# Retention and a two-layer ELU network on one Trainium2 core: the second token block's second matrix product, from one Strassen level to two

## The chip, the cores and the metric

The kernel runs on one core of a Trainium2 chip (trn2). The metric is the device time of one execution in microseconds; several executions are timed and the median is given. A profile is taken of one execution. In it, PE is TensorE (PEld its weight loads), DVE is VectorE, ACT is ScalarE, POOL is GpSimd, and SP is SyncE, which here issues all DMAs, in the order in which they stand in the program.

## The reference

Everything is fp32. First a recurrent retention over 4 sequences of 768 tokens with 8 heads of 64, then a network without biases:

```python
for t in range(S):
    state = gamma * state + outer(k[t], v[t])
    y[t] = q[t] @ state / sqrt(D)
x = y.transpose(0, 2, 1, 3).reshape(3072, 512)
h = x @ w_in                          # 512 -> 2048
g = where(h > 0, h, exp(min(h, 0)) - 1)
out = g @ w_out                       # 2048 -> 512
```

The state is one 64x64 matrix per head, gamma one number per head.

## The kernel before

**Blocks.** The 3,072 tokens are worked on in six blocks of 512, numbered 0 to 5. For each block the retention is computed in chunks (masked scores L274, states L305, outputs L339 and L365), which leaves the block's input x, turned, in `xb`. Then come the first matrix product (w_in), the ELU on ScalarE and VectorE (L419 to L423), and the second product (w_out). The retention of a block is cut into five steps (`retention_step`), which are put between the matrix products of the block before it.

**Products.** Block 0 multiplies plainly (`plain_first`, `plain_second`). Block 1 uses one Strassen-Winograd level in both products: 7 products of half-size matrices instead of 8, in the order 1, 2, 6, 7, 5, 3, 4. `first` does it for w_in, in four parts n; `second` for w_out, each product with 16 matmuls of 128x128 weights and 256 columns (32 records in the trace, since an fp32 matmul leaves two). Blocks 2 to 5 use two levels in the second product (`second_twice`: 7 x 7 = 49 products of 4 matmuls, 128 columns each, 8 records) and in two of the seven products of the first (`first_twice`).

**Weights.** They come as 16 pieces of float64 bits. `prepare` (ScalarE) and `decode` (VectorE, four operations) turn them to fp32. Pieces 0 to 7 are w_in and stay in SBUF. Pieces 8 to 15 are w_out and pass through the four slots of `w_s` while block 0 multiplies with them in `plain_second`; piece 12 takes the slot of piece 8, and so on. Pieces are loaded three ahead in a pool `stage` of three tiles: `load_piece` is called at the end of each decode. For each piece, VectorE also makes the four sums of one Strassen level, `so` (L471 to L476), and the decoded piece and `so` are stored to a DRAM scratch of 32 quarter matrices (`quarters`, L176 and L477).

**The weights of two levels.** `second` fetches each of its seven weight matrices back from that scratch (`fetch`, tile `ws`, 1 MB, three in flight, in `stage`), multiplies, and lets VectorE make the four second-level sums of the same matrix (`combine_w_out`, L594 to L600, 512 columns each), which are stored to `scratch2` for blocks 2 to 5. For w_in, GpSimd makes such sums for two matrices during block 1's first product (`combine_small`, L678, stored to `scratch3`).

**The ring.** Two-level products take their weights from a ring of 11 tiles `wq` of 256 KB; `fetch_small` issues the next fetch when a tile has been used. The ring takes the memory of the pools `stage` and `t4`, which are closed first; this is done in `change`, behind the last product of block 1's second product.

**Order.** The schedule is by hand: each engine executes its instructions in program order. Generators (`first`, `second`, ...) yield between products, and the main program decides what stands between. PSUM: banks "a" (two buffers), "b" and "d" (one each), and four for the rest. Output tiles of block 0 are in `gq["T3"]` (`g_out`), which is otherwise an input of the second product from block 1 on. The output sums of one-level products lie in `hpool`, copies of PSUM in `mpool`, four tiles each.

Of the kernel before, what the change touches and what calls it, by code (L numbers as in the profile page):

```python
# [17 lines left out]
def kernel(  # L18
# [70 lines left out]
    gq["T1"] = gq["C12"]  # L89
    four = lambda x: gq[x].rearrange("p (i a) t -> p i (a t)", a=2)  # L90
    g_plain = [four(x)[:, i, :] for x in gnames[:4] for i in range(4)]
    g_out = [gq["T3"][:, 2 * i : 2 * i + 2, :] for i in range(4)]


    chunks = [divmod(m, NCH) for m in range(NCHUNK)]
# [51 lines left out]

    quarters = lambda f: scratch.rearrange("(s k) p (f c) -> k f p s c", k=2, f=4)[f // 4, f % 4]  # L150

    def decode(fine=False):

# [305 lines left out]
    def plain_second():  # L459

        ops = [bank(x).rearrange("p a b -> p (a b)") for x in "aabd"]
        for f in range(NF):
            wo = decoded[2 * NQ + f]
            for row in range(2):
                for d in range(4):
                    nc.tensor.matmul(  # L466
                        ops[d], lhsT=wo[:, row, d * P : (d + 1) * P], rhs=g_plain[row * NF + f],
                        start=(f == 0 and row == 0), stop=(f == NF - 1 and row == 1),
                    )
            so = t4.tile([P, 4, 256], FP32, name="so", tag="t4")  # L470
            tt = lambda o, x, y, op: nc.vector.tensor_tensor(out=o, in0=x, in1=y, op=op)  # L471
            a11, a21, a12, a22 = (wo[:, r, 256 * d : 256 * d + 256] for r in range(2) for d in range(2))
            tt(so[:, 0], a21, a22, ALU.add)
            tt(so[:, 1], so[:, 0], a11, ALU.subtract)
            tt(so[:, 2], a11, a21, ALU.subtract)
            tt(so[:, 3], a12, so[:, 1], ALU.subtract)  # L476
            nc.sync.dma_start(quarters(f)[:, 8:16], so.rearrange("p a (d c) -> p (a d) c", c=P))  # L477
            yield
        for d in range(4):
            ot = g_out[d]  # L480
            eng = (nc.scalar.copy, nc.vector.tensor_copy)[d % 2]
            eng(ot.rearrange("p a b -> p (a b)"), ops[d])
            nc.sync.dma_start(out[0, d // 2, :, :, d % 2, :].rearrange("t p c -> p t c"), ot)

    def combine_w_in(n):

# [82 lines left out]
        return strassen(product, use, None)  # L569


    SLOT = {1: 0, 2: 2, 3: 7, 4: 3, 5: 4, 6: 5, 7: 6}
    ORDER2 = [1, 2, 6, 7, 5, 3, 4]
    fetched = {}

    def fetch(tb, j):
        t = stage.tile([P, 4, 4, P], FP32, name="ws", tag="stage")
        nc.sync.dma_start(
            t.rearrange("p q f c -> p q (f c)"), scratch[4 * SLOT[j] : 4 * SLOT[j] + 4].rearrange("q p x -> p q x")
        )  # L580
        fetched[tb, j] = t

    INPUT2 = {1: "C11", 2: "C21", 3: "C22", 4: "C11", 5: "T1", 6: "C11", 7: "T3"}

    def next_input(j):

        x, op = {2: ("T3", ALU.add), 6: ("C21", ALU.subtract)}[j]
        for n in range(NQ):
            q = slice(2 * n, 2 * n + 2)
            nc.vector.tensor_tensor(out=gq["C11"][:, q], in0=gq[x][:, q], in1=gq["C11"][:, q], op=op)  # L590

    def combine_w_out(j, ws):

        tt = lambda o, x, y, op: nc.vector.tensor_tensor(out=o, in0=x, in1=y, op=op)  # L594
        a11, a12, a21, a22 = (ws[:, q] for q in range(4))
        s12, s34 = (t4.tile([P, 2, 4, P], FP32, name="so", tag="t4") for _ in range(2))
        tt(s12[:, 0], a21, a22, ALU.add)
        tt(s12[:, 1], s12[:, 0], a11, ALU.subtract)
        tt(s34[:, 0], a11, a21, ALU.subtract)
        tt(s34[:, 1], a12, s12[:, 1], ALU.subtract)  # L600
        for k, x in enumerate((s12, s34)):
            nc.sync.dma_start(
                scratch2[j - 1, :, 1024 * k : 1024 * k + 1024], x.rearrange("p k f d -> p (k f d)")
            )

    def second(tb, behind_last):
        def product(j, ps, begin):
            ws = fetched.pop((tb, j))
            for f in range(NF):
                for d in range(2):  # L610
                    nc.tensor.matmul(  # L611
                        ps[:, d, :], lhsT=ws[:, 2 * d + f // 4, f % 4, :], rhs=gq[INPUT2[j]][:, f, :],
                        start=(begin and f == 0 and d == 0), stop=(f == NF - 1), skip_group_check=True,
                    )
            at = ORDER2.index(j) + 3
            if j in (2, 6):
                next_input(j)
            combine_w_out(j, ws)
            if at < 7:
                fetch(tb, ORDER2[at])  # L620
            if j == 4:
                behind_last()

        def use(name, h):
            r, t = int(name[1]) - 1, int(name[2]) - 1
            if name == "C12":
                ot = hpool.tile([P, 2, TH], FP32, name="h", tag="h")
                nc.scalar.copy(ot, h)
                h = ot
            nc.sync.dma_start(out[tb, r, t].rearrange("p d c -> p (d c)"), h.rearrange("p d c -> p (d c)"))  # L630

        return strassen(product, use, None)

    RING = 11
    TWICE = [2, 3]
    SMALL = {5: 0, 6: 1, 7: 2, 3: 3}
    small_w, to_fetch, before = [], [], []
    for tb in range(2, NTB):  # L640
        for j in TWICE:
            m1, m2, *mine = [(tb, 0, j, k) for k in (1, 2, 6, 7, 5, 4, 3)]
            to_fetch += [m1] + before[:1] + [m2] + mine[:2] + before[1:] + mine[2:3]
            before = mine[3:]
        to_fetch, before = to_fetch + before, []
        for j in ORDER2:
            last = (4, 3) if j == 4 and tb == NTB - 1 else (3, 4)
            mine = [(tb, 1, j, k) for k in (1, 2, 6, 7, 5) + last]
            to_fetch += mine[:2] + before + mine[2:5]
            before = mine[5:]  # L650
        to_fetch, before = to_fetch + before, []
    to_fetch = [x for x in to_fetch if x[1] == 1 or x[3] in SMALL]

    def fetch_small():
        if not to_fetch:
            return
        name = to_fetch.pop(0)
        _, which, j, k = name
        t = ring.tile([P, 4, P], FP32, name="wq", tag="wq")
        if k in SMALL:  # L660
            n = SMALL[k]
            nc.sync.dma_start(
                t.rearrange("p f d -> p (f d)"), (scratch3, scratch2)[which][j - 1, :, 512 * n : 512 * n + 512]
            )
        else:
            q = 4 * SLOT[j] + {1: 0, 2: 1, 4: 3}[k]
            nc.sync.dma_start(t.rearrange("p f d -> p (f d)"), scratch[q])
        small_w.append((name, t))
# [4 lines left out]
    def combine_small(j):  # L673

        t = stage.tile([P, 4, 4, P], FP32, name="wi", tag="stage")
        a11, a12, a21, a22 = (W_IN[j][:, 2 * r : 2 * r + 2, :, c, :] for r in range(2) for c in range(2))
        s1, s2, s3, s4 = (t[:, k].rearrange("p (n f) c -> p n f c", f=2) for k in range(4))
        tt = lambda o, x, y, op: nc.gpsimd.tensor_tensor(out=o, in0=x, in1=y, op=op)  # L678
        tt(s1, a21, a22, ALU.add)
        tt(s2, s1, a11, ALU.subtract)  # L680
        tt(s3, a11, a21, ALU.subtract)
        tt(s4, a12, s2, ALU.subtract)
        nc.sync.dma_start(scratch3[j - 1], t.rearrange("p k f d -> p (k f d)"))

    xs = {}

# [11 lines left out]
    def combine_x_twice():  # L698

        t = tpool.tile([P, 4, 2, 2, P], FP32, name="ts", tag="ts")  # L700
        b = [xb[:, 2 + k].rearrange("p (h t c) -> p t h c", h=2, t=2)[:, u] for k in range(2) for u in range(2)]
        for _ in quarters_of_input(t[:, :, 0], *b):
            pass
        for n, j in enumerate(TWICE):
            b11, b12, b21, b22 = (x[:, n] for x in b)
            s1, s2, s3, s4 = (t[:, k, 0, n] for k in range(4))
            xs[j] = {1: b11, 2: b21, 3: b22, 4: s4, 5: s1, 6: s2, 7: s3}
# [82 lines left out]
        return lambda: elu(g, g, 3, combine if name == "C22" else None)  # L790

    def second_twice(tb, behind_last):
        quarter = lambda x, r, t: x[:, 4 * r : 4 * r + 4, P * t : P * t + P]
        ts, kept2 = {}, {}

        def inputs(j):
# [250 lines left out]
    for n in range(NQ):  # L1047
# [14 lines left out]
        tail = cur  # L1062
        for j in smalls[n]:
            combine_small(j)
    for j in ORDER2[:3]:
        fetch(1, j)
    for m in range(2 * CPB, 3 * CPB):
        scale_v(m)

    def change():  # L1070

        nonlocal ring, tpool
        early.close()
        ring = ctx.enter_context(tc.tile_pool(name="ring", bufs=RING))
        tpool = ctx.enter_context(tc.tile_pool(name="tpool", bufs=2))
        for _ in range(RING):
            fetch_small()
        combine_x_twice()

    cur = second(1, change)  # L1080
    next(cur)
    next(cur)
    for _ in tail:
        pass
    flush()
    for step, s in enumerate(cur):
        retention_step(2, step)


    tail = iter(())  # L1090
    for tb in range(2, NTB):
        more = tb + 1 < NTB
        qa, qd, u2, end = {}, {}, {}, None
# [140 lines left out]
```

## Time and profile before

| | us |
|---|---|
| median of 5 executions | 650.88 (650.2 to 653.25) |
| the profiled execution | 653.25 |
| its span | 651.5 |
| TensorE busy | 635.2 (98%) |
| VectorE busy | 470.0 (72%) |
| ScalarE busy | 235.4 (36%) |
| GpSimd busy | 39.6 (6%) |
| mean DMA rate over the span | 206 GB/s |

The stages, as TensorE's instructions show them in the profiled execution: block 0's second product from 80.8 to 144.9, block 1's first product from there, block 1's second from 189.8 to 250.9 (with the last two products of the first and with block 2's retention between), block 2 from there to 354.3. The chain of work that ended last is followed back from the last instruction, at each step to what released it. "Issue" is time in which the engine waited for nothing that the profile shows. A line of a timeline has the start, the duration from the first start to the last end, the engine, the source line, the operation, its output and input tiles and how many instructions are merged in it; in brackets stands the idle time before it and what ended that. A window line has the bounds, the length, the busy time of TensorE, of its weight loads, VectorE, ScalarE and GpSimd with instruction counts, TensorE's clock as a share of full speed, the busy share of the DMA engines, and GB/s.

### The profile page before, as it was taken

How to read it: one execution, taken by the hardware profiler on the slowest of the kernel's cores; microseconds unless marked ns; L12 is line 12 of the kernel's file. 1: busy time of each engine (PE TensorE's matmuls, PEld its weight loads, DVE VectorE, ACT ScalarE, POOL GpSimd, SP SyncE). 2: the span in 40 equal slices, each digit the busy share in tenths (PEclk: the TensorE clock that was granted, in tenths of full speed). 3: DMA queues.
4: the chain of work that ended last, by engine and by line, in shares of the span. 5: the costliest groups of instructions: out<-in, count | busy, mean ns of one | idle time of the engine just before them, and what ended most of it. 6: DMA issues, size and time to landing. Idle time of an engine off the chain costs nothing.

```text
span 651.5 us, 15272 instructions
## 1 busy us (share of the span) xinstructions
PE 635.2 (98%) x6344; PEld 542.5 (83%) x6344; DVE 470.0 (72%) x830; ACT 235.4 (36%) x439; POOL 39.6 (6%) x38
## 2 busy tenths in 40 slices
PE   4999999999999999999989999999999999999998
PEld 3774445458888889989989988999988999988997
DVE  5689778667866636599757578958569958557976
ACT  6477542005441001546111455311355311256311
POOL 1001100000720000110000020000020000000000
PEclk9999999999999999999989999999999999999999
DMA  8648987546384766912768830688850588610694
GB/s 340 244 138 320 330 238 234 143 133 211 123 297 162 258 228 216 384 65 63 257 207 270 295 157 3 205 270 283 274 214 3 178 264 267 225 55 1 209 305 166
DMA packets 69013, 134.16 MB, mean 206 GB/s; under 512 B 5713, under 2 KB 23505, under 8 KB 66641
## 3 DMA queue, kind: packets, MB, share of 16 engines
q1 hardware_dynamic: 68944, 133.19, 60.6%
q8 instruction: 50, 0.82, 0.5%
q14 instruction: 19, 0.15, 0.1%
HBM read 109.05 MB, written 24.12 MB: 204 GB/s over the span
## 4 chain that ended last, share of the span: by engine, by line
PE 96%; DVE 1%; ACT 1%; DMA 1%; issue 1%; POOL 0%; SPq 0%; POOLq 0%
PE pa L812 16%; PE pa L773 10%; PE pd L812 8%; PE hp L452 6%; PE pa L466 4%; PE pa L611 4%; PE pb L812 4%; PE pb L773 4%; PE pa L553 4%; PE pa L727 4%; PE qa L773 3%; PE y L339 2%; PE pd L611 2%; PE qd L773 2%; PE pd L553 2%; PE pd L773 2%
## 5 line engine op out<-in xcount | busy, mean ns | idle before, releaser
L820 ACT COPY ms<-pa 128x128 f32<-128x128 f32 x83 | 22.0, 265 | 116.2 <-PE pa L812 116.2
L420 ACT ACTIVATE r<-r 128x512 f32<-128x512 f32 x96 | 60.5, 630 | 3.0
L812 PE MATMUL pa<-ts,wq 128*128 128x128 f32 x448 | 59.2, 275 | 0.0
L812 PE MATMUL pd<-ts,wq 128*128 128x128 f32 x440 | 58.2, 275 | 0.0
L812 PEld LDWEIGHTS pa<-ts,wq 128*128 128x128 f32 x448 | 54.8, 192 | 0.2
L812 PEld LDWEIGHTS pd<-ts,wq 128*128 128x128 f32 x440 | 53.5, 192 | 0.2 <-DVE res L824 0.2
L419 ACT ACTIVATE r<-gC 128x512 f32<-128x512 f32 x64 | 39.9, 624 | 33.9 <-DVE gC L781 33.9
L812 PE MATMUL pa<-gC,wq 128*128 128x128 f32 x384 | 52.2, 279 | 0.0
L812 PEld LDWEIGHTS pa<-gC,wq 128*128 128x128 f32 x384 | 47.7, 193 | 1.0
L248 POOL TENSOR_TENSOR kvn<-kvn,vf 128x512 f32<-128x512 f32 x22 | 25.6, 1168 | 359.4 <-DMA kvn<-in_qkv_dram 263.0
L423 DVE SCALAR_TENSOR_TENSOR gC<-r,gC 128x512 f32<-128x512 f32 x64 | 45.9, 749 | 0.7 <-ACT r L420 0.7
L503 ACT COPY m<-pa 128x512 f32<-128x512 f32 x27 | 15.7, 581 | 60.7 <-PE pa L611 35.5
L824 DVE TENSOR_TENSOR res<-pd,ms 128x128 f32<-128x128 f32 x54 | 15.4, 285 | 29.3 <-PE pd L812 28.7
L689 DVE TENSOR_TENSOR ts<-gC,ts 128x512 f32<-128x512 f32 x48 | 33.0, 688 | 0.8
L689 DVE TENSOR_TENSOR ts<-gC 128x512 f32<-128x512 f32 x48 | 32.8, 682 | 0.0
L466 PE MATMUL pa<-gC,w_s 128*128 128x512 f32 x64 | 30.6, 600 | 0.0
L611 PE MATMUL pa<-gC,ws 128*128 128x256 f32 x128 | 28.6, 381 | 0.0
L812 PE MATMUL pb<-gC,wq 128*128 128x128 f32 x192 | 27.3, 283 | 0.1
L611 PEld LDWEIGHTS pa<-gC,ws 128*128 128x128 f32 x128 | 24.1, 190 | 3.4
L812 PEld LDWEIGHTS pb<-gC,wq 128*128 128x128 f32 x192 | 24.5, 198 | 0.8 <-DVE gC L423 0.8
L845 ACT COPY res<-pa 128x128 f32<-128x128 f32 x27 | 7.2, 265 | 45.8 <-PE pa L812 45.8
L781 DVE TENSOR_TENSOR gC<-qa,gC 128x512 f32<-128x512 f32 x8 | 5.5, 691 | 25.1 <-PE qa L773 18.3
(206 smaller groups left out, 1298.1 us busy)
## 6 DMA issues: line engine op xcount, KB each, us to landing
wq<-scratch_dram SPq DMA_DIRECT2D x228, 256.0 KB, 4.3
wraw<-in_w_dram SPq DMA_DIRECT2D x16, 1024.0 KB, 6.0
qk<-in_qkv_dram SPq DMA_DIRECT2D x24, 512.0 KB, 7.3
kvn<-in_qkv_dram SPq DMA_DIRECT2D x24, 512.0 KB, 7.7
scratch_dram<-so SPq DMA_DIRECT2D x22, 512.0 KB, 3.4
ws<-scratch_dram SPq DMA_DIRECT2D x7, 1024.0 KB, 7.4
scratch_dram<-w_s SPq DMA_DIRECT2D x8, 512.0 KB, 7.2
out_dram<-res SPq DMA_DIRECT2D x11, 256.0 KB, 3.9
```

The lines of the kernel that those rows point to most:

```text
L248: eng.tensor_tensor(out=kv[:, 1], in0=kv[:, 1], in1=vf[:, i].unsqueeze(2).to_broadcast([C, H, D]), op=ALU.mult)
L419: nc.scalar.activation(e, h, AF.Relu, scale=-1.0)
L420: nc.scalar.activation(e, e, AF.Exp, scale=-1.0)
L423: nc.vector.scalar_tensor_tensor(g, e, -1.0, h, ALU.add, ALU.max)
L452: nc.tensor.matmul(hp, lhsT=w[n][:, fi, j // 2, j % 2, :], rhs=xb[:, j, :], start=(j == 0), stop=(j == 3))
L466: nc.tensor.matmul(ops[d], lhsT=wo[:, row, d * P : (d + 1) * P], rhs=g_plain[row * NF + f], start=(f == 0 and row == 0), stop=(f == NF - 1 ...
L553: nc.tensor.matmul(ps[:, fi, :], lhsT=w[:, fi, j2, :], rhs=x[:, j2, :], start=(begin and fi == 0 and j2 == 0), stop=(j2 == 1), skip_group_ ...
L611: nc.tensor.matmul(ps[:, d, :], lhsT=ws[:, 2 * d + f // 4, f % 4, :], rhs=gq[INPUT2[j]][:, f, :], start=(begin and f == 0 and d == 0), sto ...
L689: sub = lambda o, x, y: nc.vector.tensor_tensor(out=o, in0=x, in1=y, op=ALU.subtract)
L727: nc.tensor.matmul(ps[:, f, :], lhsT=lhs[f], rhs=xs[j][k], start=(begin and f == 0), stop=True, skip_group_check=True,)
L773: nc.tensor.matmul(ps[:, fi, :], lhsT=w[:, fi, j2, :], rhs=x[:, j2, :], start=(j in (1, 7) and fi == 0 and j2 == 0), stop=(j2 == 1), skip_ ...
L812: nc.tensor.matmul(ps, lhsT=w[:, f, :], rhs=ts[j][k][:, f, :], start=(begin and f == 0), stop=(f == 3), skip_group_check=True,)
```

## The change

Block 1's second product is done by `second_twice` as in blocks 2 to 5, with its first fetches from the ring behind block 1's first product. The second-level sums of w_out must then exist before it. They are made while block 0 decodes: `combine_w_out` takes two pieces at a time, an even and an odd one, as the two halves of the inner dimension, and makes the sums of three quarters of the decoded pieces (384 columns an operation) and of the four first-level sums `so` (512 columns). This asks for another split of the second level: by even and odd tiles of 128 rows instead of the first and the last four, in the scratch (`quarters`) and in the inputs (`quarter`). The sums of three of the four pairs lie in `mpool` and in `gq["T3"]`, of the last in two tiles of `stage`; each is stored by eight DMAs, which are put into a list and issued at set places (`send_small`). GpSimd's sums are issued from that list too. Block 0's outputs go through `hpool`. `second`, `fetch` and `change` are gone. The order of two of the seven matrices in scratch2 and the host's layout of w_out are changed to match.

```diff
-    quarters = lambda f: scratch.rearrange("(s k) p (f c) -> k f p s c", k=2, f=4)[f // 4, f % 4]
+    quarters = lambda f: scratch.rearrange("(s k) p (f c) -> k f p s c", k=2, f=4)[f % 2, f // 2]
...
             nc.sync.dma_start(quarters(f)[:, 8:16], so.rearrange("p a (d c) -> p (a d) c", c=P))
+            send_small()
+            sources = wo.rearrange("p r (d c) -> p (r d) c", d=2)[:, 1:4], so
+            if f % 2:
+                combine_w_out(f // 2, even, sources)
+            even = sources
             yield
         for d in range(4):
-            ot = g_out[d]
+            ot = hpool.tile([P, 2, TH], FP32, name="h", tag="h")
...
+    SEVEN = {1: 0, 2: 1, 4: 2, 5: 3, 6: 4, 7: 5, 3: 6}
+    to_send = []
+
+    def send_small():
+        while to_send:
+            nc.sync.dma_start(*to_send.pop(0))
+
+    def combine_w_out(at, even, odd):
+
+        tt = lambda o, x, y, op: nc.vector.tensor_tensor(out=o, in0=x, in1=y, op=op)
+        if at < 3:
+
+            ms = [mpool.tile([P, 2, TH], FP32, name="m", tag="m") for _ in range(4)]
+            ms = [m.rearrange("p a (b c) -> p (a b) c", c=P)[:, 0:3] for m in ms]
+            ss = gq["T3"].rearrange("p (k f) (b c) -> p k (f b) c", k=4, c=P)
+        else:
+            ms, ss = (stage.tile([P, 4, 4, P], FP32, name="wi", tag="stage") for _ in range(2))
+            ms = [ms[:, k, 0:3] for k in range(4)]
+        ss = [ss[:, k] for k in range(4)]
+        for first, dst, e, o in ((0, ms, even[0], odd[0]), (3, ss, even[1], odd[1])):
+            a11, a21, a12, a22 = (x[:, :, P * d : P * d + P] for x in (e, o) for d in range(2))
+            s1, s2, s3, s4 = dst
+            tt(s1, a21, a22, ALU.add)
+            tt(s2, s1, a11, ALU.subtract)
+            tt(s3, a11, a21, ALU.subtract)
+            tt(s4, a12, s2, ALU.subtract)
+            to = scratch2[first : first + dst[0].shape[1]].rearrange("j p (k f c) -> k f p j c", k=4, f=4)
+            for k in range(4):
+                to_send.append((to[k, at], dst[k]))
...
-    for tb in range(2, NTB):
-        for j in TWICE:
+    for tb in range(1, NTB):
+        for j in TWICE if tb > 1 else []:
...
-        quarter = lambda x, r, t: x[:, 4 * r : 4 * r + 4, P * t : P * t + P]
+        quarter = lambda x, r, t: x.rearrange("p (f r) c -> p r f c", r=2)[:, r, :, P * t : P * t + P]
...
         for j in smalls[n]:
             combine_small(j)
-    for j in ORDER2[:3]:
-        fetch(1, j)
+        send_small()
     for m in range(2 * CPB, 3 * CPB):
         scale_v(m)
-    def change():
-
-        nonlocal ring, tpool
-        early.close()
-        ring = ctx.enter_context(tc.tile_pool(name="ring", bufs=RING))
-        tpool = ctx.enter_context(tc.tile_pool(name="tpool", bufs=2))
-        for _ in range(RING):
-            fetch_small()
-        combine_x_twice()
-
-    cur = second(1, change)
-    next(cur)
-    next(cur)
+    early.close()
+    ring = ctx.enter_context(tc.tile_pool(name="ring", bufs=RING))
+    tpool = ctx.enter_context(tc.tile_pool(name="tpool", bufs=2))
+    for _ in range(RING):
+        fetch_small()
+
+    sec = second_twice(1, combine_x_twice)
+    for _ in range(3):
+        next(sec)
     for _ in tail:
         pass
     flush()
-    for step, s in enumerate(cur):
-        retention_step(2, step)
+    next(sec)
+    for step, s in enumerate(sec):
+        if step in (0, 1, 2, 4, 5):
+            retention_step(2, (0, 1, 2, 2, 3, 4)[step])
+        if s == ORDER2[-1]:
+            break
+    tail = sec
```

More of the change, by code (lines that the diff above doesn't have):

```diff
@@ L91 @@
     g_plain = [four(x)[:, i, :] for x in gnames[:4] for i in range(4)]
-    g_out = [gq["T3"][:, 2 * i : 2 * i + 2, :] for i in range(4)]
     chunks = [divmod(m, NCH) for m in range(NCHUNK)]
@@ L466, in plain_second @@
                     nc.tensor.matmul(
-                        ops[d], lhsT=wo[:, row, d * P : (d + 1) * P], rhs=g_plain[row * NF + f],
+                        ops[d], lhsT=wo[:, row, (d if row else d ^ 2) * P :][:, 0:P], rhs=g_plain[row * NF + f],
                         start=(f == 0 and row == 0), stop=(f == NF - 1 and row == 1),
@@ L471, in plain_second @@
             tt = lambda o, x, y, op: nc.vector.tensor_tensor(out=o, in0=x, in1=y, op=op)
-            a11, a21, a12, a22 = (wo[:, r, 256 * d : 256 * d + 256] for r in range(2) for d in range(2))
+            a21, a11, a12, a22 = (wo[:, r, 256 * d : 256 * d + 256] for r in range(2) for d in range(2))
             tt(so[:, 0], a21, a22, ALU.add)
@@ L569, in first @@
         return strassen(product, use, None)
-    SLOT = {1: 0, 2: 2, 3: 7, 4: 3, 5: 4, 6: 5, 7: 6}
+    SLOT = {1: 1, 2: 2, 3: 7, 4: 3, 5: 4, 6: 5, 7: 6}
     ORDER2 = [1, 2, 6, 7, 5, 3, 4]
[L574 to L581, printed above, removed]
     INPUT2 = {1: "C11", 2: "C21", 3: "C22", 4: "C11", 5: "T1", 6: "C11", 7: "T3"}
@@ L590, in next_input @@
             nc.vector.tensor_tensor(out=gq["C11"][:, q], in0=gq[x][:, q], in1=gq["C11"][:, q], op=op)
[L592 to L632, printed above, removed]
     RING = 11
@@ L662, in fetch_small @@
             nc.sync.dma_start(
-                t.rearrange("p f d -> p (f d)"), (scratch3, scratch2)[which][j - 1, :, 512 * n : 512 * n + 512]
+                t.rearrange("p f d -> p (f d)"), (scratch2[SEVEN[j]] if which else scratch3[j - 1])[:, 512 * n : 512 * n + 512]
             )
@@ L682, in combine_small @@
         tt(s4, a12, s2, ALU.subtract)
-        nc.sync.dma_start(scratch3[j - 1], t.rearrange("p k f d -> p (k f d)"))
+        to_send.append((scratch3[j - 1], t.rearrange("p k f d -> p (k f d)")))
     xs = {}
@@ L1085 @@
     flush()
-    for step, s in enumerate(cur):
-        retention_step(2, step)
-    tail = iter(())
+    next(sec)
[5 more added lines that the diff above has]
+    tail = sec
     for tb in range(2, NTB):
@@ L1216 @@
     w_in = w_in.reshape(2, 2, 128, 2, 4, 2, 128).transpose(4, 3, 2, 5, 0, 1, 6).reshape(8, 128, 1024)
-    w_out = w_out.reshape(2, 8, 128, DM).transpose(1, 2, 0, 3).reshape(8, 128, 2 * DM)
+    w_out = w_out.reshape(2, 8, 128, 2, DM // 2)
+    w_out = _np.stack([w_out[0][:, :, ::-1], w_out[1]]).transpose(1, 2, 0, 3, 4).reshape(8, 128, 2 * DM)
     w_bits = _np.concatenate([w_in, w_out], axis=0).view(_np.uint64)
```

## The prediction

> **What bounds the kernel now.** I read the page first: the busy shares and the chain of work that ended last.
>
> ```profile
> span 651.5 us, 15272 instructions
> ...
> PE 635.2 (98%) x6344; PEld 542.5 (83%) x6344; DVE 470.0 (72%) x830; ACT 235.4 (36%) x439; POOL 39.6 (6%) x38
> ...
> PE 96%; DVE 1%; ACT 1%; DMA 1%; issue 1%; POOL 0%; SPq 0%; POOLq 0%
> ```
>
> TensorE works 98% of the span and carries 96% of the chain. So the time is the sum of matmul issue times, plus whatever new gap appears between them. A matmul's duration is no price, since they overlap; I read the spacing of starts in the timeline of TensorE, the second GEMM of block 1 (L611) and of block 2 (L812):
>
> ```profile
> 189.84 7.07 PE L611 MATMUL pa<-gC,ws 128*128 128x256 f32 x32
> 196.74 1.89 PE L553 MATMUL pa<-xb,w_s 128*128 128x256 f32 x8
> ...
> 311.32 1.06 PE L812 MATMUL pa<-ts,wq 128*128 128x128 f32 x8
> 312.21 1.06 PE L812 MATMUL pd<-ts,wq 128*128 128x128 f32 x8
> ```
>
> A one-level product of 32 matmul records takes 6.90 us until the next start, a two-level product of 8 takes 0.89.
>
> Then the timeline of VectorE at the end of block 0, where its added work goes, and the windows by stage for the DMA share:
>
> ```profile
> 88.20 0.42 DVE L471 TENSOR_TENSOR so<-w_s 128x256 f32<-128x256 f32 x1
> ...
> 89.67 0.69 DVE L163 TENSOR_SCALAR wraw<-wraw 128x1024 f32<-128x1024 f32 x1
> ...
> 143.43 0.69 DVE L482 COPY gT<-pa 128x512 f32<-128x512 f32 x1 [4.43 <-PE pa L466]
> 145.15 0.69 DVE L482 COPY gT<-pd 128x512 f32<-128x512 f32 x1 [1.03 <-PE pd L466]
> ...
> 146.47 0.69 DVE L393 TENSOR_TENSOR xt<-xb,xt 128x512 f32<-128x512 f32 x1
> ```
>
> ```profile
> 104.00:108.00 4.00, 4.00 (x114) 2.74 (x107) 2.81 (x7) 2.13 (x3) 0.00 (x0) 1.00 0.82 223
> 108.00:112.00 4.00, 4.00 (x11) 1.85 (x10) 3.89 (x7) 0.47 (x1) 0.00 (x0) 1.00 0.97 297
> 112.00:132.00 20.00, 20.00 (x276) 10.42 (x276) 12.99 (x23) 2.34 (x2) 0.00 (x0) 1.00 0.48 135
> ```
>
> In each window line the last two figures are DMA share and GB/s. VectorE has a few gaps at the end of block 0; the DMA engines are nearly full until 112 and half empty after.
>
> [...] the fetches of the small weights must wait for landings, as the ws fetches here do: the third is held until about 183.7, when the store issued at 178.61 has landed (5.0 us). [...] while GpSimd works (166 to 178), VectorE operations of 0.69 us take up to 1.7.
>
> **The change part by part.**
>
> *TensorE.* Out: 7 products of L611. Their starts span 6.90, 7.00, 7.11, 7.10, 7.10, 7.11 and 7.01 us, sum 49.33. In: 49 products of 8. At 0.893 each they are 43.76; start to start, with the retention steps between them, blocks 3 and 4 each take 44.63, block 2 takes 46.26 (a 2.32 us issue gap at 329.96 and 3.4 us of half clock follow one another there). I take 44.63: **-4.7**, between -5.6 and -3.1. Retention's matmuls are placed otherwise, but are the same.
>
> *Ring start moves.* The ring of 11 small tiles opens before block 1's second GEMM instead of behind it. Today its first fetches (251.06) race with block 2's first products: the 112 L727 starts there take 13.14 us, at 112.6 ns elsewhere 12.6. **-0.5** (0 to -0.6).
>
> *VectorE in block 0.* Per pair of decoded pieces four operations of 384 and four of 512 are added. Four of 256 (L471) take 1.47 us start to start, four of 512 (L594) 2.54, so four of 384 about 2.0: 4.55 a pair, 18.2 in all. 28 operations of L594 (7 x 2.54 = 17.8 us) leave block 1, where VectorE was not the bound: worth nothing. The added ones delay what stands behind them in VectorE's queue. With the durations of the trace: pair 0 ends 94.2; decode of piece 11 (3.9 us) 98.1; masks 2.4, sums 1.5, piece 12 at 105.9; states 2.7; pair 1 ends 114.5; piece 13 ends 118.4 (its matmuls start 123.0); piece 14 ends 124.0 (131.1); pair 2 ends 130.2; piece 15 ends 134.1 (138.1). So every decoded piece is still in time, the last by 4 us. Then xb 136.5, sums 138.0, L487 140.8, sums 142.2, pair 3 ends 146.8, two PSUM copies 148.0, xt[1] at 149.4. Block 1's third product (start 148.40 today) needs xt[1]: TensorE waits **1.05 us**. The idle 4.43 and 1.03 us before the copies are used up by this; the lag is gone by 154.4, where VectorE idles 1.66 us today.
>
> *Waits on stores.* m and T3 are reused, so pairs 1 and 2 wait until the stores of pairs 0 and 1 have landed. A pair is 3,584 packets of 512 B; such packets take 28 ns here, so 6.3 us of all 16 engines. Pair 0's eight stores go out at 102.4 to 105.6; DMA is 0.71 to 0.97 busy until 112, so they land by some 108 to 113, where pair 1 needs them from 110 on. Pair 1's leave from 120.6 to 123.8 (SyncE holds them behind a store that needs piece 13 and the sums of 120.1), share 0.48 there; needed from 125.7 to 129.5. A landing takes 3.2 us median for so, 8.7 at most: the wait is 0 to 2.5 us. I take **+0.45**. SyncE's queue: piece 15's load slips from 103.7 to 106, needed by ScalarE at 114; ScalarE's preparation of piece 14 waits for pair 1 to 111.9, needed at 120. Both are hidden by the 4 us above and cost one for one beyond it. Output tiles now come from hpool; their stores land by about 152, the sums that reuse them start at 150.9, 155 and later.
>
> *Head of block 1's second GEMM.* GpSimd's eight operations end at 178.6, their store lands at 183.6, the first fetch leaves at 184 and lands after 3.1 us (the quickest of the cold burst at 251; median 7.0, as eight queue up). First tile 187, needed at 189.84; second 188, needed at 190.7; the third only at 195.1. **0**, with 2.9 us of cover. C21, the second input, is ready at 198.7, needed at 199.8.
>
> *Inside it.* VectorE is in order, and bank d has one buffer: a product that starts in d waits for the addition that reads the last one. Masks (2.4 us) and state sums (2.7) now stand ahead of two such additions, first()'s last sum ahead of a third: 0.2 + 0.3 + 0.3 = **+0.8** by the same walk, at most the 5.1 us of both.
>
> Sum: -4.7 - 0.5 + 1.05 + 0.45 + 0.8 = -2.9 us. The profiled execution took 653.25 us (span 651.5 and 1.75 around it), the slowest of five, whose median is 650.88. So 650.35 for one like the profiled, **648.0** from the median.
>
> **Rivals.** *VectorE's lag eats the gain.* The landings take 2.5 us, the two-level stage loses 2 us more to bank d. For it: shares of 0.82 to 0.97 where pair 0's stores go, and one VectorE queue for all. Against it: half-empty DMA after 112, and blocks 3 and 4, where VectorE carries most of the same load with no gap. The waits are then 1.05 + 2.5 + 2.0 = 5.5 against 5.2 gained: about 651, within 649.6 to 652.8.
>
> *The ring starts late (slower).* One mechanism at the head of block 1's second GEMM: TensorE waits for the first fetches, these for the store of the last sums of w_in, these for GpSimd. Each microsecond later than 187 + 2.9 is a microsecond of TensorE; at 5.8 us late the gain is gone, at 7.8 it is slower by 0.3%. For it: cold landings of 7.0 us median and 8.1 at most; if the first product is held by such a landing and GpSimd and its store slip by 5 to 8 us (VectorE is late[...]), the delay is 9 to 12 us. Then 651 to 654; with a half clock after so long a gap (3.4 us at half cost 1.7 today) 653 to 656, middle 654. Against it: nothing in the trace makes GpSimd so late.
>
> *It doesn't do what it says.* Excluded: in the order of instructions the 224 records of L611 are replaced by 392 of two-level ones.
>
> **How the numbers follow.** This kernel's measurement can't tell less than 0.3%, 1.95 us, from no change. Forecast: 0.58 (645.8 to 649.8; its spread is the -5.6 to -3.1 and the 0 to 2.5). VectorE's lag: 0.24. Ring late, with unseen waits of its kind: 0.18. Below 648.93: four fifths of the forecast, 0.46. Above 652.83: nearly all of the ring's case and a sliver of the lag's, 0.19. Between: 0.35. The range 645.8 to 653.8 leaves out a twentieth below and about 0.12 above.
>
> **What would show it.** Right: two-level matmuls in block 1 start to start 44 to 46 us without retention; a single gap of 1 to 2 us before the third product of block 1 (xt the releaser); no DMA releasing TensorE at block 1's first two-level product; L727 of block 2 near 12.6. Wrong: gaps by w_s decode in block 0, waits of VectorE on scratch stores above 3 us, or a DMA-released gap at 190.

## The result: a little slower

| | before | after |
|---|---|---|
| median, us | 650.17 (646.71 to 654.75) | 652.16 (650.03 to 653.66) |
| ratio after/before | | 1.0024, 95% interval 1.0015 to 1.0033 |
| profiled execution, us | 653.25 | 650.23 |
| its span, us | 651.5 | 648.0 |

The change costs about 1.6 us by the ratio (the medians differ by 2.0) where 2.9 were to be gained. On two chips, in the companion runs below, the ratio was 1.0037 (1.0023 to 1.0051) and 1.0056 (1.0038 to 1.0074). The two profiles say the opposite, 3.5 us less span. So the first reading lesson of this case is that the spans of two single executions can't be subtracted; stages can.

The page of the kernel after: span, busy time, and the chain by engine.

```profile
span 648.0 us, 15834 instructions
...
PE 629.1 (97%) x6512; PEld 542.6 (84%) x6512; DVE 494.0 (76%) x887; ACT 240.8 (37%) x463; POOL 39.0 (6%) x38
...
PE 68%; DVE 8%; DMA 2%; POOL 1%; SPq 1%; issue 1%; ACT 0%; DVEq 0%; POOLq 0%
```

TensorE has lost 6 us of busy time, but VectorE now carries 8% of the chain, where it had 1%. (The shares printed come to 81%, so this chain is a pointer and no account.) The timeline of TensorE shows the first place where it waits for VectorE, in block 1's first product (L588, L553 before), and further down the new two-level products that answer to L611. Here xt is the tile of the four sums of quarters of x that the one-level product needs; gC stands for the quarters C11 to C22 of its result.

```profile
144.93 1.89 PE L588 MATMUL pb<-xb,w_a 128*128 128x256 f32 x8
148.77 2.98 PE L588 MATMUL pa<-xt,w_s 128*128 128x256 f32 x8 [1.95 <-DVE xt L392]
151.54 2.61 PE L588 MATMUL pd<-xt,w_s 128*128 128x256 f32 x8
153.98 1.89 PE L588 MATMUL pa<-xt,w_b 128*128 128x256 f32 x8
...
191.97 1.05 PE L797 MATMUL pa<-gC,wq 128*128 128x128 f32 x8
...
199.63 1.16 PE L797 MATMUL pa<-ts,wq 128*128 128x128 f32 x8 [0.32 <-ACT ms L805]
```

The third product before, without a wait:

```profile
148.40 1.89 PE L553 MATMUL pa<-xt,w_s 128*128 128x256 f32 x8
```

Before, a product here is followed by the next after 1.73 us (146.67 to 148.40). After the change, TensorE is idle for 1.95 us ahead of the third, which starts 2.11 us late, and then it and the fourth take 2.77 and 2.44 us to the next start. VectorE's timeline shows why the third is late, and the windows of the same stretch (after the bounds stand the length and TensorE's busy time; the third figure from the right is TensorE's granted clock, then DMA share and GB/s) why the next two are long.

```profile
145.41 0.69 DVE L499 TENSOR_TENSOR wi<-so,wi 128x512 f32<-128x512 f32 x1
146.01 0.69 DVE L486 COPY h<-pa 128x512 f32<-128x512 f32 x1
146.61 0.68 DVE L486 COPY h<-pd 128x512 f32<-128x512 f32 x1
147.21 0.68 DVE L392 TENSOR_TENSOR xt<-xb 128x512 f32<-128x512 f32 x1
147.93 0.69 DVE L392 TENSOR_TENSOR xt<-xb,xt 128x512 f32<-128x512 f32 x1
```

```profile
112.00:132.00 20.00, 20.00 (x230) 10.20 (x220) 18.76 (x33) 2.51 (x3) 0.00 (x0) 1.00 1.02 297
...
148.00:150.00 2.00, 1.23 (x5) 1.10 (x6) 2.00 (x4) 0.00 (x0) 0.00 (x0) 0.89 1.03 332
150.00:152.00 2.00, 2.00 (x7) 1.56 (x6) 1.93 (x4) 1.47 (x3) 0.00 (x0) 0.50 1.08 311
152.00:154.00 2.00, 2.00 (x9) 1.69 (x8) 1.81 (x3) 0.37 (x1) 0.00 (x0) 0.76 0.90 166
```

The last sums of w_out (wi, L499) end at 146.1, two PSUM copies follow, and xt[1] is ready at 148.6. VectorE has hardly any idle time left between 112 and 132 (18.76 of 20 us busy, 12.99 before), and the DMA engines are full there (share 1.02, 0.48 before). TensorE's clock is at half for some 3.4 us from about 149.6 on: (0.11 + 0.50 + 0.24) x 2 = 1.7 us are lost to it.

The second place is in each of the blocks 2 to 5. The timeline of TensorE at the second product of block 2, after:

```profile
305.42 0.83 PE L797 MATMUL pa<-gC,wq 128*128 128x128 f32 x6
306.94 0.49 PE L797 MATMUL pa<-gC,wq 128*128 128x128 f32 x2 [0.69 <-DVE gC L422]
```

the operation of VectorE that it waits for:

```profile
306.20 0.68 DVE L422 SCALAR_TENSOR_TENSOR gC<-r,gC 128x512 f32<-128x512 f32 x1
```

and the first two products of C21 before:

```profile
307.46 1.06 PE L812 MATMUL pa<-gC,wq 128*128 128x128 f32 x8
308.35 1.34 PE L812 MATMUL pb<-gC,wq 128*128 128x128 f32 x8
```

with the same operation of VectorE:

```profile
308.24 0.68 DVE L423 SCALAR_TENSOR_TENSOR gC<-r,gC 128x512 f32<-128x512 f32 x1
```

After, the first product of the second input C21 stops ahead of its last two matmuls and waits 0.69 us for L422, the last operation of the ELU (VectorE, 306.20 to 306.88). Start to start (the next product starts at 307.26) it takes 1.84 us where 0.89 is usual, so 0.95 are lost. Before, the product ran through, and only the next lost something: it took 1.34 instead of 1.06 us, 0.28, since its fifth matmul starts at 308.98, behind the end of L423 at 308.92. The difference is 0.67 a block. In `second_twice` the first half of C21 is tiles 0 to 3 before, and tiles 0, 2, 4, 6 after. Tile 6 belongs to n = 3, the last that the first product delivers.

To take the stages apart, I read from each trace the start of the first matmul of: block 0's first product, its second, block 1's first, block 1's second, and the second product of blocks 2, 3, 4 and 5. The differences, and what is left to the last matmul:

| profile | bl. 0 first | bl. 0 second | bl. 1 first | bl. 1 second to bl. 2 second | to bl. 3 | to bl. 4 | to bl. 5 | rest |
|---|---|---|---|---|---|---|---|---|
| before | 61.77 | 64.15 | 44.89 | 111.43 | 104.67 | 100.40 | 95.98 | 45.94 |
| after | 60.27 | 64.15 | 48.76 | 107.26 | 101.07 | 101.34 | 96.66 | 46.61 |

Chance is seen in block 0's first product and, before, between blocks 2 and 3 (the issue gap and half clock told of in the prediction). The change is seen in three columns: block 1's first product +3.9, block 1's second -4.2, and +0.67 in each of the blocks 2 to 5 (100.40 to 101.07 where no issue gap falls, 95.98 to 96.66, 45.94 to 46.61), 2.7 together.

### The profile page after: what moved, and what is told of

The parts are those of the page before. It is cut to its first block, busy times and chain, and to the rows that moved or that the text cites. A ratio compares the mean times of both kernels' runs of the same rounds, so it can differ in the third digit from the quotient of the medians.

```text
span 648.0 us, 15834 instructions
## 1 busy us (share of the span) xinstructions
PE 629.1 (97%) x6512; PEld 542.6 (84%) x6512; DVE 494.0 (76%) x887; ACT 240.8 (37%) x463; POOL 39.0 (6%) x38
## 4 chain that ended last, share of the span: by engine, by line
PE 68%; DVE 8%; DMA 2%; POOL 1%; SPq 1%; issue 1%; ACT 0%; DVEq 0%; POOLq 0%
PE pa L797 18%; PE pa L758 10%; PE pd L797 9%; PE pb L797 5%; PE pa L712 4%; PE pb L758 4%; PE qa L758 3%; PE pd L712 2%; PE qd L758 2%; PE pd L758 2%; DVE gC L422 1%; POOL wi L663 1%; PE y L338 1%; PE pa L588 1%; PE sc L273 1%
## 5 line engine op out<-in xcount | busy, mean ns | idle before, releaser
L797 PE MATMUL pa<-ts,wq 128*128 128x128 f32 x560 | 74.1, 275 | 0.3 <-ACT ms L805 0.3
L797 PE MATMUL pd<-ts,wq 128*128 128x128 f32 x552 | 73.2, 276 | 0.0
L797 PEld LDWEIGHTS pa<-ts,wq 128*128 128x128 f32 x560 | 68.5, 192 | 0.8 <-ACT ms L805 0.5
L797 PE MATMUL pa<-gC,wq 128*128 128x128 f32 x480 | 65.9, 279 | 2.9 <-DVE gC L422 2.8
L797 PEld LDWEIGHTS pd<-ts,wq 128*128 128x128 f32 x552 | 67.2, 192 | 0.4 <-DVE res L809 0.2
L797 PEld LDWEIGHTS pa<-gC,wq 128*128 128x128 f32 x480 | 59.3, 192 | 4.9 <-DVE gC L422 3.5
L422 DVE SCALAR_TENSOR_TENSOR gC<-r,gC 128x512 f32<-128x512 f32 x64 | 42.5, 696 | 0.7 <-ACT r L419 0.7
L674 DVE TENSOR_TENSOR ts<-gC,ts 128x512 f32<-128x512 f32 x60 | 41.2, 687 | 1.0
L674 DVE TENSOR_TENSOR ts<-gC 128x512 f32<-128x512 f32 x60 | 41.0, 683 | 0.2
L758 PE MATMUL pa<-xt,w_s 128*128 128x256 f32 x96 | 23.0, 382 | 0.0
L758 PE MATMUL pa<-xt,w_b 128*128 128x256 f32 x96 | 23.0, 382 | 0.0
```

The costliest lines, as they stand in the source:

```text
L422: nc.vector.scalar_tensor_tensor(g, e, -1.0, h, ALU.add, ALU.max)
L674: sub = lambda o, x, y: nc.vector.tensor_tensor(out=o, in0=x, in1=y, op=ALU.subtract)
L758: nc.tensor.matmul(ps[:, fi, :], lhsT=w[:, fi, j2, :], rhs=x[:, j2, :], start=(j in (1, 7) and fi == 0 and j2 == 0), stop=(j2 == 1), skip_ ...
L797: nc.tensor.matmul(ps, lhsT=w[:, f, :], rhs=ts[j][k][:, f, :], start=(begin and f == 0), stop=(f == 3), skip_group_check=True,)
```

## The experiments

Three theories were open. *The split* (even and odd tiles make blocks 2 to 5 wait). *VectorE's lag* (added work ahead of xt makes block 1's third product late). *Chance* (these gaps belong to the one profile).

### Both kernels again

> The changed kernel again, as the companion of the three variants on this chip. Theory (the split costs blocks 2 to 5 some 3 us, VectorE's lag costs block 1 some 4): 1 to 2 us slower than before, ratio 1.0015 to 1.003, with the 0.7 us waits on gC in blocks 2 to 5 and the 2 us wait on xt at block 1's third product again. Rival (the profiled execution had these gaps by chance): one of them absent in this second profile.

> The kernel before once more, for a second trace of it. If the issue gap of 2.3 us and the half clock in block 2 of the first profile were chance, they are not in the same place here, and block 2 takes about 100.5 us from its first two-level product of the second kind to block 3's, as block 3 does, and not 104.7.

> The changed kernel, as the companion of these two on the same chip: 1.5 to 3 us slower than before, with the wait on xt and the four waits on gC.

After, on two chips: 653.24 against 650.40, and 653.11 against 649.75, ratios given above. Before, a single execution: 647.9. The stages, and the wait on xt:

| profile | bl. 0 first | bl. 1 first | wait on xt | bl. 1 second to bl. 2 second | to bl. 3 | to bl. 4 | to bl. 5 | rest |
|---|---|---|---|---|---|---|---|---|
| before, 2nd trace | 60.73 | 44.89 | none | 111.60 | 100.41 | 100.41 | 95.99 | 45.94 |
| after, 2nd trace | 62.54 | 47.09 | 1.82 | 107.54 | 101.07 | 101.59 | 98.78 | 46.62 |
| after, 3rd trace | 60.25 | 49.25 | 2.43 | 107.53 | 101.07 | 101.89 | 96.65 | 46.61 |

Chance falls as the cause: each trace of the kernel after has the wait on xt and the four of 0.7 us on gC, and both of before are alike to 0.01 us in block 1's first product. The event of 4.3 us in block 2 of the first profile of before was chance, as expected: 100.41 here. The stages of after above 101.07 and 96.66 (101.34 to 101.89, 98.78) hold issue gaps of 0.1 to 1.8 us, which differ from trace to trace. What was chance in block 0's first product shows in TensorE's timeline of after (first line) and in that of its second trace: the same 16 matmuls.

```profile
18.78 3.72 PE L440 MATMUL pa<-xb,w_a 128*128 128x256 f32 x16 [0.92 <-DVE xb L373]
```

```profile
19.22 6.12 PE L440 MATMUL pa<-xb,w_a 128*128 128x256 f32 x16 [0.64 <-DVE xb L373]
```

These 2.4 us are in some executions and not in others, and the traces tell why: TensorE's granted clock is first recorded as full at 16.45 in the one and at 24.11 in the other. In the first trace of before, where that is at 22.36, these matmuls start 0.43 us apart from 19.61 to 22.17 and 0.22 apart from 22.48 on. With the full clock from 16.45, 22.36 and 24.11 on, block 0's first product takes 60.27, 61.77 and 62.54 us. The first profile of after looked better than that of before by the event of 4.3 us in block 2 of before, and by 1.5 us of this.

### The split alone, on the kernel before

```diff
-    quarters = lambda f: ...[f // 4, f % 4]
+    quarters = lambda f: ...[f % 2, f // 2]
...
-                        ps[:, d, :], lhsT=ws[:, 2 * d + f // 4, f % 4, :], ...
+                        ps[:, d, :], lhsT=ws[:, 2 * d + f % 2, f // 2, :], ...
...
-        quarter = lambda x, r, t: x[:, 4 * r : 4 * r + 4, P * t : P * t + P]
+        quarter = lambda x, r, t: x.rearrange("p (f r) c -> p r f c", r=2)[:, r, :, P * t : P * t + P]
```

> The kernel before with the even/odd split alone: block 1's second product stays at one level. Theory (with even and odd tiles, the first product of the second input needs the last tiles of C21, so TensorE waits once in each of the blocks 2 to 5): 2.3 to 3.4 us slower than before, that is 652.5 to 653.6 where before takes 650.2, with four waits of about 0.7 us on gC and 45.3 to 45.6 us for the two-level second product of blocks 3 and 4 instead of 44.6. Rival (the split is free, the whole loss comes from VectorE's lag in block 1): equal to before within 0.5 us.

651.93 against 650.40, ratio 1.0029 (1.0012 to 1.0045): 1.9 us slower, between 0.8 and 2.9. The waits of TensorE in this kernel (us in total, times, longest) have the row of the kernel after:

```profile
PE pa L812 <- DVE gC L423: 2.8, 4, 0.7
```

Blocks 2 to 5 take 101.08, 101.07, 96.66 and 46.62, the kernel after's figures to 0.01, and block 1's first product the 44.89 of before. So the split alone is enough for this loss, 0.67 x 4 = 2.7 us in the trace. The median shows a little less, within its interval.

### The changed kernel without the split

```diff
-                        ..., rhs=g_plain[row * NF + f],
+                        ..., rhs=g_plain[row * NF + f // 2 + 4 * (f % 2)],
...
-        quarter = lambda x, r, t: x.rearrange("p (f r) c -> p r f c", r=2)[:, r, :, P * t : P * t + P]
+        quarter = lambda x, r, t: x[:, 4 * r : 4 * r + 4, P * t : P * t + P]
...
-    w_out = w_out.reshape(2, 8, 128, 2, DM // 2)
+    w_out = w_out.reshape(2, 8, 128, 2, DM // 2)[:, [0, 4, 1, 5, 2, 6, 3, 7]]
```

A pair of pieces in succession is now tiles 0 and 4, 1 and 5 and so on, so that the pairwise sums stay possible with halves.

> The changed kernel with the split back at the first and the last four tiles: w_out's pieces come in the tile order 0, 4, 1, 5, 2, 6, 3, 7, so that a pair of pieces is still one row of both halves. Theory (split): 2.3 to 3.4 us faster than the changed kernel, so 0.5 to 2 us faster than before, and the waits on gC gone in blocks 2 to 5. Rival (lag alone): equal to the changed kernel within 0.5 us, about 1.5 us slower than before.

> The variant with the first and the last four tiles alone, again, beside the others on one chip. Theory: 2.3 to 3.4 us faster than the changed kernel and 2 to 4 us slower than the variant with the spread sums and the stores' new order. Its wait on the ring at 224.8 of 1.3 us, if it was chance, is not in this trace.

649.79 against 653.24 of the kernel after on the same chip, and 649.25 against 653.11 on another: 3.5 and 3.9 us faster, a little more than the trace's 2.7. So the split is not only enough for the loss, but needed for it. Against before, 0.9997 (0.9980 to 1.0013) and 0.9986 (0.9969 to 1.0004). The waits on gC are gone from both traces, and the stages to block 3 and to block 5 are back at 100.41 and 95.98 or 95.99. The wait on the ring was 1.3 us in the first trace and 0.5 in the second; no trace of the kernel after has one at this place, nor have the two variants further down that build on this one. Its cause was not looked for. The wait on xt stays (2.73 and 2.08 us), as does block 1's first product at 49.55 and 48.90: the two causes are separate.

### The last pair's sums behind xt

```diff
-            if f % 2:
+            if f % 2 and f < 7:
                 combine_w_out(f // 2, even, sources)
+            elif f == 7:
+                last_pair.append((even, sources))
...
     combine_x()
+    combine_w_out(3, *last_pair.pop())
```

> The changed kernel with the sums of the last pair of pieces moved behind the making of block 1's inputs xt on VectorE. Theory (VectorE's lag makes block 1's third product late by 2 us, and TensorE's clock is halved right after this gap, for some 1.8 us more): 2 to 3.9 us faster than the changed kernel, no wait on xt at that product, 45 us from block 1's first matmul to its first two-level one instead of 48.8. Rival (the half clock comes anyway, and the wait moves to a later addition on VectorE): 0 to 1 us faster.

654.39 against 653.24, 1.2 us above the kernel after, which six executions do not set apart from it (1.0038 to 1.0082 of before, against 1.0023 to 1.0051). The expected gain did not come, nor the small one of the rival, though the wait moved as the rival said. TensorE's timeline, VectorE's and ScalarE's show where the wait went:

```profile
150.86 1.89 PE L591 MATMUL pd<-xt,w_s 128*128 128x256 f32 x8
156.08 2.97 PE L591 MATMUL pa<-xt,w_b 128*128 128x256 f32 x8 [3.34 <-ACT m L541]
```

```profile
152.94 0.68 DVE L502 TENSOR_TENSOR wi<-so,wi 128x512 f32<-128x512 f32 x1
153.55 0.68 DVE L546 TENSOR_TENSOR h<-pb,m 128x512 f32<-128x512 f32 x1
```

```profile
154.26 0.63 ACT L418 ACTIVATE r<-h 128x512 f32<-128x512 f32 x1 [6.08 <-DVE h L546]
154.93 0.63 ACT L419 ACTIVATE r<-r 128x512 f32<-128x512 f32 x1
155.46 0.57 ACT L541 COPY m<-pa 128x512 f32<-128x512 f32 x1
```

The third and the fourth product start on time, but the eight sums now stand ahead of the first addition of block 1. ScalarE, in order, waits for that addition before it copies bank "a" for the third product, and the fifth product waits for the bank. That is a second place for VectorE's lag, with its deadline: the addition has to start 2.5 us before the fifth product is due, that is 4.4 us after block 1's start. Behind the gap the fifth and the sixth product take 5.25 us in place of 3.46, with a mean granted clock of 0.92 from 140 to 160, and the first product takes 50.18 us.

### Two copies to ScalarE

```diff
-            eng = (nc.scalar.copy, nc.vector.tensor_copy)[d % 2]
-            eng(ot.rearrange("p a b -> p (a b)"), ops[d])
+            nc.scalar.copy(ot.rearrange("p a b -> p (a b)"), ops[d])
```

> The changed kernel with the two PSUM copies of block 0's outputs that VectorE does (0.6 us each, between the last sums and the making of xt) given to ScalarE, which is idle there for 22 us. Theory (the wait on xt is VectorE's lag, one for one, and a half clock may follow it): the wait falls from 1.9 to about 0.7 us, 1.2 us faster than the changed kernel, up to 3 us where the half clock no longer follows. Rival (as with the last pair moved, the wait goes to another addition on VectorE): the sum of TensorE's waits in block 1's first product stays near 2 us, and the time within 0.5 us.

651.19 against 650.30, ratio 1.0017 (0.9997 to 1.0038). TensorE's waits:

```profile
PE pa L587 <- ACT m L537: 1.0, 1, 1.0
...
PE pa L587 <- DVE xt L392: 0.6, 1, 0.6
```

The wait on xt fell as forecast, one for one; 1.05 us came back at the place that the experiment before had shown. The sum is 1.7, near the 1.8 to 2.4 of the kernel after, so the rival holds for the waits. No half clock followed (granted clock 1.00 from 144 to 160): block 1's first product takes 47.10. The interval includes the changed kernel's 1.0024, so no gain is claimed from this run.

This second wait was not VectorE's lag any more: the addition L542 began at 149.59 after 1.14 us of idle, put down to the store of the output tile h.

### Spread: halves, copies on ScalarE, xt first, two sums later

The edits of the halves and of the copies, and:

```diff
     combine_x()
+    for _ in range(3):
+        next(last_pair[0])
...
         for _ in tail:
             pass
+        if n == 0:
+            for _ in last_pair[0]:
+                pass
```

with `combine_w_out` as a generator of four steps of two sums each.

> The variant with first and last four tiles, and VectorE's lag taken off both places that waited: block 0's output copies all on ScalarE, xt made ahead of the last pair's sums, and of these eight sums the last two made only behind the first addition of block 1. Theory (both causes are separate and add up): no wait on xt, m or gC of more than 0.5 us; 44.9 to 45.5 us from block 1's first matmul to its first two-level one; 2 to 4 us faster than the variant with the halves alone, 645.5 to 647.5, so 3 to 5 us faster than before. Rival (the gain of two levels is lost in a further wait): at 649 to 650, with a new wait in the trace.

649.80 against 650.30, ratio 0.9984 (0.9971 to 0.9997): faster than before, but by 1.0 us where 3 to 5 were expected. Over the halves alone (0.9997 and 0.9986) no gain is shown. The theory missed a wait, as the rival said: 2.0 us on m at the fifth product. VectorE's line and SyncE's timeline (time, issue time, queue) show it:

```profile
152.55 0.69 DVE L548 TENSOR_TENSOR h<-pb,m 128x512 f32<-128x512 f32 x1 [2.35 <-DMA out_dram<-h]
```

```profile
140.54 3.20 SPq L498 DMA_DIRECT2D scratch_dram<-m  x4
143.78 3.19 SPq L498 DMA_DIRECT2D scratch_dram<-gT  x4
147.08 0.81 SPq L476 DMA_DIRECT2D scratch_dram<-so  x1
147.99 4.15 SPq L489 DMA_DIRECT2D out_dram<-h  x4
```

The addition writes a tile of `hpool` that has just held an output of block 0, and so waits until that output's store has landed. ScalarE made that tile at 144.2, but SyncE was busy until 147.9, with the eight small stores of pair 2, which stand behind the store of so for tile 6 and with it wait for VectorE until 140.1.

### And the stores in another order

```diff
+            send_small()
             nc.sync.dma_start(quarters(f)[:, 8:16], so.rearrange("p a (d c) -> p (a d) c", c=P))
-            send_small()
```

> The spread variant (halves again, output copies on ScalarE, xt ahead of the last sums) with one more edit: a pair's eight stores are issued ahead of the next piece's store of so instead of behind it. In the spread variant the wait that is left (2.0 us on m) goes back to SyncE: pair 2's eight stores occupy it from 140.5 to 147.0, so the first output store leaves only at 148.0, and the first addition of block 1 waits 2.35 us for its tile. Theory (SyncE's queue of small stores is the second limit behind VectorE's lag): pair 2's stores leave by about 141, the output stores at 145, no wait above 0.5 us in block 1's first product, 44.9 to 45.3 us from block 1's first matmul to its first two-level one, and 2 us faster than the spread variant: 647 to 648.5, ratio to before 0.995 to 0.9975. Rival (the store that lands late is late for the DMA engines' load and not for the queue): the addition still waits until about 152, and the time is that of the spread variant.

646.42 against 649.75, ratio 0.9947 (0.9930 to 0.9963): 3.4 us faster than before, and 2.8 us faster than the halves alone on the same chip (649.25). This version beats both kernels. What the new order gives without the spread sums was not run. SyncE's timeline and VectorE's:

```profile
135.52 3.20 SPq L498 DMA_DIRECT2D scratch_dram<-m  x4
138.77 3.19 SPq L498 DMA_DIRECT2D scratch_dram<-gT  x4
...
144.18 4.80 SPq L489 DMA_DIRECT2D out_dram<-h  x4
```

```profile
149.66 0.69 DVE L548 TENSOR_TENSOR h<-pb,m 128x512 f32<-128x512 f32 x1 [0.65 <-PE pb L593]
```

The small stores leave 5 us earlier, the output stores nearly 4, and the addition now waits for TensorE and for nothing else. The rival falls: the DMA engines are no less full than in the spread variant (share 0.98 to 0.99 from 136 to 148, 0.46 to 1.01 there), and the addition no longer waits for a store. Block 1's first product takes 44.89 us, the figure of before to the last digit; block 1's second to block 2's takes 107.41; blocks 2 to 5 100.41, 100.41, 95.99 and 45.95. So in the trace the gain from block 1's second product to block 2's is left whole, 111.60 - 107.41 = 4.2 us, of which the medians show 3.4 (2.4 to 4.5).

## Why the prediction was wrong

The three traces of after, against the second of before:

| step | forecast, us | measured, us |
|---|---|---|
| block 1's second product, waits inside, start of the ring (-4.7, +0.8, -0.5) | -4.4 | -4.1 to -4.3 |
| wait for xt[1], and the landings of the stores (+1.05, +0.45) | +1.5 | +2.2, +3.9, +4.4 |
| ring cold start | 0 | 0 |
| blocks 2 to 5 | 0 | +2.7 |
| sum | -2.9 | +0.8 to +3.0 |

**The step that failed is one that the prediction never wrote.** Its sum has no term for blocks 2 to 5, and it gives no reason for putting them at nothing. The diff's line `quarter` changes which tiles each of their products reads, and the walk through the parts should have asked, for the first product of C21, when its last input is ready. The answer stood in the profile of before: the product behind it already had a gap of 0.28 us inside, so the last tile came just in time for the second half of C21, and the split brings that tile one product forward. Four losses of 0.95 us in place of four of 0.28 cost 2.7 us. The runs with the split alone and without it show this; by itself it turns the forecast of -2.9 into no change.

**Mis-sized: VectorE's lag.** Place, releaser and mechanism were as told, and the traces hold the single gap before block 1's third product. The gap is 1.8 to 2.4 us, where 1.05 and 0.45 were written down separately. The four pairs of sums hold VectorE for 19.3 to 19.7 us in the three traces, where 18.2 and 0.45 were told; 0.5 to 0.8 of it are named as waits for landings of scratch stores. In the profile of after, sums of 384 take 548 to 560 ns and sums of 512 take 682 to 693; the first four of 384 take 2.00 us start to start (87.93 to 89.93), as the estimate had it. What was left out is the half clock behind the gap, 1.75 us in two of three traces, and this is the larger part of the miss there. The prediction priced a half clock only for the ring's rival.

**Missed, but hidden here: the landing of the output stores.** The prediction has both numbers, "land by about 152" and the sum that reuses a tile at 150.9, and drew no wait from them. Eight small stores were to leave SyncE in 3.2 us; in the profile of after they take 7.8, 6.7 and 6.4. The DMA engines, told half empty, were full (share 1.02 from 112 to 132, 0.99 from 140 to 144): pair 2's eight stores carry 1.8 MB (four of 192 KB, four of 256), and at 6.4 us that is 287 GB/s, while the engines move 285 in the windows where their share is 0.99 to 1.00. So it is not shown whether issuing or moving sets these 6.4 us; in the spread variant a store of so takes SyncE 0.36 us ahead of them (140.13) and 0.81 behind them (147.08), for the same bytes. In the kernel after VectorE comes to the addition at 149.78, just behind the landing at 149.65, so there is no wait. It came out as soon as VectorE was quicker, and made two variants fall short, the copies on ScalarE and the spread one.

**Right.** The two-level matmuls of block 1's second product take 45.7 to 46.0 us start to start (44 to 46 told), L712 of block 2 takes 12.60 in the three traces of after (12.6 told, 13.14 and 13.31 before), no DMA holds the first two-level product, and block 0's second product takes 64.15 us in all twelve traces: every decoded piece is in time although VectorE has 19 us more to do. One of these hits may be luck: the kernel with the split alone, whose ring starts as before, also takes 12.60 there (L727), so the 0.5 us are not shown to come from the ring's start. The ring's rival did not happen. The rival of VectorE's lag named the outcome nearest to the truth, about 651, but with other terms: landings and the waits inside the two-level stage were to cost 4.5 us, and cost 1.5 to 2.2 (0.5 to 0.8 of landings, and 45.7 to 46.0 against 44.63).

## What to carry to other kernels

A change of layout or of the order of tiles is a change to every consumer of that layout: for each, ask which tile its first instruction needs last, and when that one is made. When an engine in order falls behind, there is a row of deadlines behind the first one that is missed (here xt, then the addition that frees a bank, then the store that frees its tile); removing the first shows the second, so list them all with their times before moving work. Many small stores held up what stood behind them in SyncE's queue: eight took 6.4 us with the DMA engines full, and letting them go first took away the last 2 us of waiting (47.16 to 44.89 in block 1's first product).

## Of the hardware, not expected

Gaps of TensorE of about 2 us were followed by 3.4 us of half clock in some of these traces and not in others, at a cost of 1.75 us that did not grow with the gap. In block 1's first product of the eight traces that have a gap there, the two products behind it took 5.2 us instead of 3.46 after gaps of 1.95, 2.08, 2.43, 2.73 and 3.34 us, and 3.56 to 3.57 after 1.05, 1.82 and 2.00 (granted clock 1.00 throughout, from 140 to 160 or from 144 to 160). So the length of the gap didn't decide alone: 1.95 us cost 1.75 more, and 2.00 cost 0.1. The record of the granted clock shows where the half clock fell.

In the profile of after it begins at 149.57 and lasts 3.413 us. The clock is first recorded as full at 16.45, which is 133.12 us before, or 39.0 times 3.413. In the profile of before it begins at 332.98 and lasts 3.413 us too, 310.61 us after the clock is first full at 22.36, or 91.0 times. I therefore divided both profiles into stretches of this length from the first full clock on. That of after has 3.42 - 1.47 = 1.95 us without a matmul in one stretch, and the next is at half clock:

```profile
146.15:149.57 3.42, 1.47 (x8) 1.00 (x7) 3.38 (x6) 0.00 (x0) 0.00 (x0) 1.00 1.01 311
149.57:152.98 3.41, 3.41 (x10) 2.70 (x9) 3.31 (x6) 1.84 (x3) 0.00 (x0) 0.50 1.05 268
```

In its second trace a bound at 150.40 (37.0 times 3.413 behind 24.11) parts the gap of 1.82 us into 0.87 and 0.94, and the clock stays full:

```profile
146.99:150.40 3.41, 2.54 (x12) 1.90 (x10) 3.41 (x6) 0.59 (x1) 0.00 (x0) 1.00 1.03 284
150.40:153.81 3.41, 2.47 (x12) 2.21 (x13) 3.34 (x7) 0.69 (x2) 0.00 (x0) 1.00 1.01 327
```

In the profile of before, the stretch ahead of the half clock (329.57 to 332.98) has 3.41 - 1.09 = 2.32 us without a matmul. No other stretch of the two profiles up to the last matmul has more than 1.02, and behind none of the others the clock is halved. That is what these traces show; whether the same holds for other gaps, and how much idle time in a stretch is enough, no run here was made to find.
